# Two PSUM copies of q moved from VectorE to ScalarE, with another instruction order, in a fused attention and gated convolution kernel

## The chip, the cores and the metric

The kernel runs on one core of one Trainium2 chip. The metric is the device time of one execution in microseconds, as the median of several runs. All five engines of the core take part: TensorE (PE), VectorE (DVE), ScalarE (ACT), GpSimd (POOL), which only starts loads, and SyncE (SP), which only starts stores and the small copies through DRAM.

## The reference, cut to what matters

Eight batches, eight heads of 64 columns, 576 positions. First a linear attention without softmax, with an RMS norm per head; its result is the input of a feed-forward part with a convolution over positions and a gate:

```
kv  = einsum('bhsd,bhse->bhde', k, v)
o   = einsum('bhsd,bhde->bhse', q, kv)
o   = o / sqrt(mean(o*o, -1) + 1e-6) * g_norm          # per head
x   = o, heads side by side                            # (8, 576, 512)
h   = max(x @ w_in, 0)                                 # (8, 576, 1024)
c   = sum over k of conv_w[k] * h shifted by k-1       # 3 taps over positions
out = (h * sigmoid(c)) @ w_out                         # (8, 576, 512)
```

## The kernel before

The work is cut into some 660 small steps, each a function marked `@op` and named by two to four letters. A string `ORDER` lists all steps by name and numbers, such as `hm.3.2`; the kernel calls them in that order, and at the end ties every instruction to its predecessor on the same engine. So the string fixes the order on each engine and in each DMA queue, and semaphores do the rest: an engine that comes to a step whose input or buffer isn't ready waits, and everything behind it on that engine waits too. The strings are written out by a search outside of the kernel.

The steps, for batch b, pair of heads t (0 to 3), block f of 128 of the 1024 columns (0 to 7), with the engine of each:

- `Lq`, `Lk`, `Lv` (POOL) start the loads of a batch, two buffers each. Batch 0 is loaded in parts ahead of the order's steps.
- `qs` and `qt` (PE) transpose q into PSUM, `qs` one pair of batch 0, `qt.b.u` two pairs of a later batch; `qd` and `qc.b.u` copy the result to SBUF. These copies are of 128 x 576 and 128 x 1152 elements in bf16.
- `kv` (PE) multiplies k and v, and `kvc` copies the halves of the product into a block-diagonal matrix: on DVE for batch 0, on ACT for the others.
- `ot` (PE) makes o for a pair; `sq` (ACT) squares it and `oc` copies it to SBUF in the order of positions (ACT, for batch 0 mostly DVE).
- The norm. Batch 0: `on` (PE), `nl`, `nx` (ACT), `mu0` (DVE), pair by pair. Other batches, in the groups 1 (batch 1), 2 (batches 2 and 3), 3 (4 and 5), 4 (6 and 7): `ss` (PE) sums squares, `ln` and `ex` (ACT) give 1/rms. For groups 1 and 2, `sl` (DVE) splits it into bf16 parts, `sp` (PE) spreads it over partitions in PSUM and `mu` (DVE) multiplies. For groups 3 and 4 it goes through DRAM: `rw` (SP) writes it, `rr` (SP) reads it back spread over partitions, in two DMAs into one of four buffers rb, and `mr` (DVE) multiplies.
- `hm.b.f` (PE; `hs` its first three quarters) makes a block of h from all four pairs, `re` (ACT) applies the relu. `ws` (DVE) casts w_in, `cs` and `cm` (DVE) make constants for the norm.
- The convolution: `ta` and `ad` (DVE) make the taps and add them, `sg` (ACT) the sigmoid, `mg` (DVE) the gate. Two blocks of batch 0 have it on PE: `di`, `sv` (ACT), `cv` (PE), `mv` (DVE).
- `om.p.m` (PE) multiplies 128 rows of the pair p of batches with w_out, `ea` (ACT) copies the result to SBUF, `st` (SP) stores it.
- `wu.n` and `wa.n` (PE) are n matmuls of zeros which fill a wait.

PSUM has two pools. Pool a has three buffers of two banks and serves `ot`, `on`, `qt`, `hs`/`hm`, `sp`, `cv` and `wa`; pool b has two of one bank and serves `qs`, `kv`, `ss`, `om` and `wu`. A step on PE that takes a buffer waits for the last reader of what was in it.

Where a copy runs is decided by one function, from a default and from two tuples of exceptions, `ON_ACT` and `ON_DVE`:

```python
    def copy(token, on_dve, to, fr):
        if token in ON_DVE or on_dve and token not in ON_ACT:
            nc.vector.tensor_copy(to, fr)
        else:
            nc.scalar.activation(to, fr, AX.Copy)
```

Some lines of the profile are those of helpers: L237 and L239 are the DVE and the ACT copy above, L232 the load of an ACT table, L157 a load, L361 `qt`, L393 the larger matmul of `ot` and `on`, L435 `sq`, L510 `ln`, L526 `ex`, L554 `mu`, L571 `rr`, L580 `mr`, L595 `hm`, L608 `re`, L628 `ta`, L643 `sg`, L649 `mg`, L703 `om`, L710 `ea`, L721 `st`.

Of the kernel before, what the change touches and what calls it, by code (L numbers as in the profile page):

```python
# [65 lines left out]
ONES, KEEP, XB, RD, SQO, PW, ON_ACT, ON_DVE = ({0: (0, 1, 2, 3)}, ((0, 2), (0, 3)), (), (), (), (), ('oc.0.0',), ())  # L66

ORDER = """
cvq wu.11 qs.0.0 qd.0.0 cvk kv.0.0.1 kvc.0.0.1.0 kvc.0.0.1.1 cs wa.3 ot.0.0 oc.0.0 qs.0.1 kv.0.1.1 sq.0.0 wa.2
on.0.0 nl.0.0 kvc.0.1.1.1 kvc.0.1.1.0 qd.0.1 qs.0.2 wu.1 kv.0.2.1 qd.0.2 kvc.0.2.1.0 kvc.0.2.1.1 ot.0.1 wu.1  # L70
ot.0.2 sq.0.2 oc.0.1 nx.0.0 sd.0.1 wu.3 on.0.2 nl.0.2 Lq.1 nx.0.2 kv.0.3.1 mu0.0.0 kvc.0.3.1.0 kvc.0.3.1.1
qs.0.3 qd.0.3 on.0.1 nl.0.1 wa.4 ot.0.3 sq.0.3 mu0.0.2 cx cz ws.0 nx.0.1 mu0.0.1 wu.2 on.0.3 nl.0.3 nx.0.3
mu0.0.3 wu.5 hs.0.0 hs.0.1 hm.0.0 hm.0.1 re.0.1 re.0.0 Lk.1.0 Lv.1.0 Lk.1.1 ws.1 hm.0.2 hm.0.3 Lv.1.1 Lw Lq.2
Lk.2.2 re.0.2 ws.2 di.1 hm.0.7 qt.1.0 re.0.7 re.0.3 di.0 hm.0.6 re.0.6 hm.0.4 kv.1.0.2 qc.1.0 kvc.1.0.2.1
kvc.1.0.2.0 cm ta.0.2 re.0.4 hm.0.5 re.0.5 ot.1.1 sq.1.1 oc.1.1 ta.0.3 Lv.2.2 ad.0.1 qt.1.1 ot.1.0 oc.1.0
kv.1.2.2 kvc.1.2.2.1 cv.0.1 kvc.1.2.2.0 ta.0.6 qc.1.1 sq.1.0 ot.1.3 sq.1.3 ot.1.2 ta.0.7 ad.0.3 sq.1.2 wu.4
ss.1 oc.1.3 ln.1 ex.1 ta.0.4 sl.1 cv.0.0 ta.0.5 sv.0.0 sv.0.1 oc.1.2 wu.10 sp.1.0 mu.1.0 sp.1.1 sp.1.3 mu.1.1
mu.1.3 qt.2.1 sp.1.2 mu.1.2 qt.2.0 sg.0.1 sg.0.3 mg.0.3 qc.2.0 ad.0.2 hm.1.6 hm.1.7 re.1.6 qc.2.1 sg.0.2
mg.0.2 hm.1.4 hm.1.5 re.1.7 kv.2.0.4 re.1.5 kvc.2.0.4.0 kvc.2.0.4.1 re.1.4 hm.1.0 mg.0.1 ta.1.6 ta.1.7 mv.0.0
Lq.3 Lk.3.2 Lv.3.2 Lq.4 Lk.4.2 ot.2.3 oc.2.3 sq.2.3 hm.1.3 re.1.3 qt.3.1 re.1.0 ot.2.0 ot.2.1 oc.2.0 oc.2.1  # L80
ad.1.3 qc.3.1 sq.2.0 hm.1.2 ot.2.2 sq.2.1 qt.3.0 oc.2.2 sq.2.2 re.1.2 kv.3.0.4 hm.1.1 kvc.3.0.4.1 kvc.3.0.4.0
ot.3.2 re.1.1 ta.1.4 mv.0.1 ta.1.5 ad.1.2 qc.3.0 ot.3.1 sq.3.2 oc.3.2 sq.3.1 om.0.1 ta.1.2 ot.3.0 Lv.4.2
oc.3.1 ot.3.3 qt.4.1 sq.3.0 ss.2 ta.1.3 ad.1.1 sq.3.3 ss.3 qc.4.1 ea.0.1 ta.1.0 ta.1.1 ln.2 qt.4.0 qc.4.0
om.0.0 ex.2 om.0.3 sl.2 oc.3.3 oc.3.0 ea.0.0 ea.0.3 Lq.5 Lk.5.2 Lv.5.2 Lq.6 sp.2.0 sp.3.2 mu.2.0 sp.2.2 mu.3.2
mu.2.2 kv.4.0.4 sg.1.1 sg.1.3 sp.2.1 sp.2.3 om.0.2 sp.3.0 mu.2.3 mu.2.1 mg.1.1 kvc.4.0.4.1 mu.3.0 sp.3.3
hm.2.0 hm.2.3 sg.1.2 re.2.0 kvc.4.0.4.0 mu.3.3 Lk.6.2 mg.1.3 re.2.3 ea.0.2 sp.3.1 mu.3.1 hm.2.2 mg.1.2 re.2.2
ad.1.0 ot.4.0 sq.4.0 hm.3.2 oc.4.0 qt.5.1 kv.5.0.4 qc.5.1 re.3.2 sg.1.0 hm.3.3 kvc.5.0.4.0 ot.4.3 qt.5.0
re.3.3 ta.2.2 sq.4.3 hm.3.1 Lv.6.2 oc.4.3 kvc.5.0.4.1 mg.1.0 re.3.1 ot.4.1 qc.5.0 sq.4.1 oc.4.1 hm.3.0 hm.2.6
ta.2.3 ad.2.1 Lq.7 ot.5.2 re.3.0 re.2.6 hm.2.1 hm.2.7 oc.5.2 sq.5.2 re.2.1 ot.4.2 re.2.7 hm.3.6 st.0.2 oc.4.2
sq.4.2 hm.3.7 ta.2.0 ta.2.1 re.3.6 re.3.7 ot.5.3 hm.3.5 ot.5.0 sq.5.3 st.0.3 st.0.0 st.0.1 Lk.7.2 Lv.7.2  # L90
# [689 lines left out]
```

## Time and profile before

| | before |
|---|---|
| median of 3 runs (lowest to highest) | 189.31 us (189.17 to 190.07) |
| the profiled execution's own time | 190.19 us |
| its span in the profile | 187.9 us |
| PE busy | 178.5 us |
| DVE busy | 159.4 us |
| ACT busy | 150.2 us |
| moved by DMA | 32.35 MB |
| granted TensorE clock | 0.999 |

Busy time is the time in which an engine executes an instruction; matmuls overlap their successors in the record, so PE's figure is not a share of its peak. Rows of groups read: line, engine, operation, tiles, shapes, count, then total busy us and mean ns of one, then the idle time in front of them and what ended it. The chain that ended last is followed back from the last instruction, at each step to what released it; its rows are start, us, engine, tile and line. All times are from the start of the span.

### The profile page before, as it was taken

The page shows a single profiled execution, that of the slowest core. Times are in us where ns is not written, and L with a number is a line of the kernel's source. Part 1 is how long each engine was busy: PE and PEld are TensorE (multiplying, and loading weights), DVE is VectorE, ACT ScalarE, POOL GpSimd, SP SyncE. Part 2 cuts the span into 40 slices and gives each one's busy share as a digit, 9 for nine tenths or more (in the row PEclk, how much of TensorE's full clock was granted, in tenths as well). Part 3 has the DMA queues.
Part 4 walks back from the last instruction along what each step waited for, and adds up shares of the span by engine and source line. Part 5 has one row for each costly group of instructions (what it writes and reads, how often), then busy time and mean ns, then how long its engine had stood idle before and what let it go on. Part 6 is the DMA issues. An engine that isn't in the chain of part 4 may idle for free.

```text
span 187.9 us, 4432 instructions
## 1 busy us (share of the span) xinstructions
PE 178.5 (95%) x1787; PEld 108.0 (57%) x1787; DVE 159.4 (85%) x324; ACT 150.2 (80%) x233; POOL 29.3 (16%) x42
## 2 busy tenths in 40 slices
...
GB/s 147 183 265 332 203 205 204 206 202 203 204 204 203 207 200 238 265 205 128 118 178 196 198 131 61 0 89 262 161 232 178 98 81 3 108 128 129 166 195 167
DMA packets 30876, 32.35 MB, mean 172 GB/s; under 512 B 1776, under 2 KB 25864, under 8 KB 30856
## 3 DMA queue, kind: packets, MB, share of 16 engines
...
q14 instruction: 6, 0.05, 0.1%
...
## 4 chain that ended last, share of the span: by engine, by line
PE 47%; ACT 25%; DMA 9%; DVE 8%; SPq 4%; issue 2%; POOL 2%; ACTq 0%; POOLq 0%; DVEq 0%
PE om_ps L703 20%; PE h_ps L595 19%; ACT h L608 7%; DMA rb<-scr 6%; ACT sq L435 6%; ACT o L239 5%; SPq L571 3%; DMA v_sb<-in_v_dram 3%; PE kv_ps L319 2%; DVE h L649 2%; ACT L232 2%; ACT row L710 2%; DVE xT L580 2%; PE qt_ps L361 1%; DVE xT L554 1%
## 5 line engine op out<-in xcount | busy, mean ns | idle before, releaser
L595 PE MATMUL h_ps<-xT,w_in_sb 128*128 128x288 bf16 x512 | 68.4, 286 | 1.7 <-DVE xT L580 0.6
L703 PE MATMUL om_ps<-w_out_sb,h 128*128 128x512 bf16 (+1 forms) x296 | 64.4, 373 | 0.0
L595 PEld LDWEIGHTS <-w_in_sb 128*128 128x128 bf16 x512 | 49.3, 98 | 18.6 <-issue 4.1
L703 PEld LDWEIGHTS <-h 128*128 128x128 bf16 x296 | 28.5, 98 | 31.7 <-DVE h L649 0.3
L608 ACT ACTIVATE h<-h_ps 128x576 bf16<-128x576 f32 x64 | 40.1, 656 | 7.0 <-PE h_ps L595 6.6
L628 DVE TENSOR_SCALAR side<-h,cw 128x576 bf16<-128x576 bf16 (+1 forms) x92 | 38.2, 427 | 1.0
L643 ACT ACTIVATE tap<-tap 128x1152 bf16<-128x1152 bf16 (+1 forms) x23 | 34.1, 1496 | 2.3 <-DVE tap L637 2.3
L710 ACT ACTIVATE row<-om_ps 128x512 f32<-128x512 f32 (+1 forms) x37 | 21.5, 586 | 14.9 <-PE om_ps L703 13.6
L637 DVE TENSOR_TENSOR tap<-tap,side 128x1150 bf16<-128x1150 bf16 (+1 forms) x23 | 22.4, 973 | 0.8
L649 DVE TENSOR_TENSOR h<-h,tap 128x1152 bf16<-128x1152 bf16 (+1 forms) x23 | 21.6, 962 | 0.6 <-ACT tap L643 0.6
L636 DVE TENSOR_TENSOR tap<-tap,side 128x1150 bf16<-128x1150 bf16 (+1 forms) x23 | 22.1, 961 | 0.0
L435 ACT ACTIVATE sq<-o_ps 128x576 bf16<-128x576 f32 x31 | 19.7, 662 | 1.9 <-PE o_ps L393 1.9
L239 ACT ACTIVATE o<-o_ps 128x576 f32<-128x576 f32 x29 | 18.5, 657 | 1.8 <-PE o_ps L393 1.8
L628 DVE TENSOR_SCALAR tap<-h,cw 128x576 bf16<-128x576 bf16 (+1 forms) x46 | 19.3, 421 | 0.0
L580 DVE TENSOR_TENSOR xT<-o,rb 128x576 bf16<-128x576 f32 x16 | 12.0, 755 | 2.2 <-DMA rb<-scr 2.1
L237 DVE COPY qT<-qt_ps 128x1152 bf16<-128x1152 bf16 x14 | 10.5, 753 | 3.0 <-PE qt_ps L361 3.0
L728 PE MATMUL wu_ps<-zeros 128*128 128x512 bf16 x37 | 11.6, 454 | 1.2 <-DVE zeros L184 1.2
L157 POOL DMA_DIRECT2D q_sb<-in_q_dram x10 | 7.6, 756 | 33.1 <-PE qt_ps L361 32.2
L393 PE MATMUL o_ps<-qT,kvbd 128*128 128x512 bf16 x32 | 11.7, 379 | 0.0
L157 POOL DMA_DIRECT2D k_sb<-in_k_dram x11 | 9.1, 828 | 11.7 <-PE kv_ps L319 9.0
L361 PEld LDWEIGHTS <-q_sb 96*64 96x64 bf16 x336 | 8.3, 110 | 3.8 <-issue 3.4
L361 PE MATMUL qt_ps<-ident,q_sb 96*64 96x96 bf16 x336 | 9.6, 207 | 0.5 <-DVE xT L554 0.2
...
## 6 DMA issues: line engine op xcount, KB each, us to landing
...
```

Source lines behind the costliest of these rows:

```text
L239: nc.scalar.activation(to, fr, AX.Copy)
L361: nc.tensor.transpose(ps[i * D:(i + 1) * D, tt, r * PS:(r + 1) * PS], q_sb[:, 2 * (2 * u + tt) + i, r * D:(r + 1) * D], ident[:PS, :PS])
L435: nc.scalar.activation(to, fr, AX.Square)
L595: nc.tensor.matmul(ps[:, e, :HS], w_in_sb[:, t, f * P:(f + 1) * P], x[:, t, e * HS:(e + 1) * HS], start=(t == 0), stop=(t == NT - 1))
L608: nc.scalar.activation(h_tile(b // 2)[:, f, b % 2, :].rearrange("p (e n) -> p e n", e=2), T["hm", b, f][:, :, :HS], AX.Relu)
L628: nc.vector.tensor_scalar_mul(tap[m][:, f % 2, :, :].rearrange("p b s -> p (b s)"), h_tile(p)[:, f, bs, :].rearrange("p b s -> p (b s)"), ...
L636: nc.vector.tensor_add(tap[:, :, 1:], tap[:, :, 1:], side[:, 0, :, :S - 1])
L637: nc.vector.tensor_add(tap[:, :, :S - 1], tap[:, :, :S - 1], side[:, 1, :, 1:])
L643: nc.scalar.activation(tap, tap, AX.Sigmoid)
L649: nc.vector.tensor_mul(h, h, T["tap", c, j])
L703: nc.tensor.matmul(to, h[:, f, m * P:(m + 1) * P], w_out_sb[:, f, cols], start=(f == 0), stop=(f == NF - 1))
L710: nc.scalar.activation(T["os", p, m][:, cols], fr, AX.Copy)
```

## The change

Two tokens are added to `ON_ACT`, so that the copies `qc.1.0` and `qc.1.1` (128 x 1152 bf16, PSUM to SBUF) are ACT instructions and no longer DVE instructions. The whole `ORDER` is another one: nearly the same steps (only the fillers `wu` and `wa` are cut up differently: 37 matmuls in `wu` and 9 in `wa` before, 42 and 4 after), in other places. Two new tuples, `F32` and `OM_A`, are empty. The parts of the order that the text below speaks of:

```diff
-ONES, KEEP, XB, RD, SQO, PW, ON_ACT, ON_DVE = ({0: (0, 1, 2, 3)}, ((0, 2), (0, 3)), (), (), (), (), ('oc.0.0',), ())
+ONES, KEEP, XB, RD, SQO, PW, ON_ACT, ON_DVE, F32, OM_A = ({0: (0, 1, 2, 3)}, ((0, 2), (0, 3)), (), (), (), (), ('oc.0.0', 'qc.1.0', 'qc.1.1'), (), (), ())
 
 ORDER = """
-cvq wu.11 qs.0.0 qd.0.0 cvk kv.0.0.1 kvc.0.0.1.0 kvc.0.0.1.1 cs wa.3 ot.0.0 oc.0.0 qs.0.1 kv.0.1.1 sq.0.0 wa.2
-on.0.0 nl.0.0 kvc.0.1.1.1 kvc.0.1.1.0 qd.0.1 qs.0.2 wu.1 kv.0.2.1 qd.0.2 kvc.0.2.1.0 kvc.0.2.1.1 ot.0.1 wu.1
-ot.0.2 sq.0.2 oc.0.1 nx.0.0 sd.0.1 wu.3 on.0.2 nl.0.2 Lq.1 nx.0.2 kv.0.3.1 mu0.0.0 kvc.0.3.1.0 kvc.0.3.1.1
-qs.0.3 qd.0.3 on.0.1 nl.0.1 wa.4 ot.0.3 sq.0.3 mu0.0.2 cx cz ws.0 nx.0.1 mu0.0.1 wu.2 on.0.3 nl.0.3 nx.0.3
-mu0.0.3 wu.5 hs.0.0 hs.0.1 hm.0.0 hm.0.1 re.0.1 re.0.0 Lk.1.0 Lv.1.0 Lk.1.1 ws.1 hm.0.2 hm.0.3 Lv.1.1 Lw Lq.2
-Lk.2.2 re.0.2 ws.2 di.1 hm.0.7 qt.1.0 re.0.7 re.0.3 di.0 hm.0.6 re.0.6 hm.0.4 kv.1.0.2 qc.1.0 kvc.1.0.2.1
-kvc.1.0.2.0 cm ta.0.2 re.0.4 hm.0.5 re.0.5 ot.1.1 sq.1.1 oc.1.1 ta.0.3 Lv.2.2 ad.0.1 qt.1.1 ot.1.0 oc.1.0
-kv.1.2.2 kvc.1.2.2.1 cv.0.1 kvc.1.2.2.0 ta.0.6 qc.1.1 sq.1.0 ot.1.3 sq.1.3 ot.1.2 ta.0.7 ad.0.3 sq.1.2 wu.4
-ss.1 oc.1.3 ln.1 ex.1 ta.0.4 sl.1 cv.0.0 ta.0.5 sv.0.0 sv.0.1 oc.1.2 wu.10 sp.1.0 mu.1.0 sp.1.1 sp.1.3 mu.1.1
-mu.1.3 qt.2.1 sp.1.2 mu.1.2 qt.2.0 sg.0.1 sg.0.3 mg.0.3 qc.2.0 ad.0.2 hm.1.6 hm.1.7 re.1.6 qc.2.1 sg.0.2
...
-Lq.3 Lk.3.2 Lv.3.2 Lq.4 Lk.4.2 ot.2.3 oc.2.3 sq.2.3 hm.1.3 re.1.3 qt.3.1 re.1.0 ot.2.0 ot.2.1 oc.2.0 oc.2.1
-ad.1.3 qc.3.1 sq.2.0 hm.1.2 ot.2.2 sq.2.1 qt.3.0 oc.2.2 sq.2.2 re.1.2 kv.3.0.4 hm.1.1 kvc.3.0.4.1 kvc.3.0.4.0
-ot.3.2 re.1.1 ta.1.4 mv.0.1 ta.1.5 ad.1.2 qc.3.0 ot.3.1 sq.3.2 oc.3.2 sq.3.1 om.0.1 ta.1.2 ot.3.0 Lv.4.2
-oc.3.1 ot.3.3 qt.4.1 sq.3.0 ss.2 ta.1.3 ad.1.1 sq.3.3 ss.3 qc.4.1 ea.0.1 ta.1.0 ta.1.1 ln.2 qt.4.0 qc.4.0
-om.0.0 ex.2 om.0.3 sl.2 oc.3.3 oc.3.0 ea.0.0 ea.0.3 Lq.5 Lk.5.2 Lv.5.2 Lq.6 sp.2.0 sp.3.2 mu.2.0 sp.2.2 mu.3.2
-mu.2.2 kv.4.0.4 sg.1.1 sg.1.3 sp.2.1 sp.2.3 om.0.2 sp.3.0 mu.2.3 mu.2.1 mg.1.1 kvc.4.0.4.1 mu.3.0 sp.3.3
...
-oc.5.3 re.3.5 sq.5.0 ss.4 ot.5.1 hm.2.4 sq.5.1 ss.5 oc.5.0 om.0.7 ad.2.0 re.2.4 ta.2.6 ta.2.7 ad.2.3 hm.3.4
-ln.3 ex.3 oc.5.1 hm.2.5 re.3.4 rw.3 ea.0.7 re.2.5 st.0.7 qt.6.0 qt.6.1 sg.2.3 rr.4.0 om.0.4 ea.0.4 om.0.8
-ea.0.8 ta.2.4 ta.2.5 ad.2.2 qc.6.1 qt.7.1 sg.2.1 kv.6.0.4 om.0.6 mr.4.0 qt.7.0 rr.4.2 qc.6.0 kvc.6.0.4.1
-mr.4.2 kvc.6.0.4.0 kv.7.0.4 ea.0.6 rr.4.1 sg.2.2 mr.4.1 qc.7.0 rr.4.3 mr.4.3 qc.7.1 ot.6.2 mg.2.3 rr.5.0
...
-sq.6.1 re.5.7 ot.7.2 oc.6.1 ad.3.0 ea.1.5 sq.7.2 ss.6 st.1.0 re.5.4 hm.4.4 re.4.4 ss.7 ln.4 ex.4 hm.5.5 hm.5.2
-om.1.7 re.5.5 hm.5.3 ta.3.6 ta.3.7 oc.7.2 ad.3.3 ta.3.4 hm.4.3 re.5.2 hm.4.2 om.1.2 sg.3.3 ta.3.5 ad.3.2
-ea.1.7 mg.3.3 rw.4 rr.6.0 rr.6.2 st.1.5 st.1.7 rr.6.3 re.4.2 ta.3.2 re.5.3 om.1.4 ea.1.2 re.4.3 om.1.3 ea.1.4
-mr.6.0 ta.3.3 sg.3.0 st.1.4 ea.1.3 mr.6.2 rr.6.1 st.1.3 om.1.8 ea.1.8 sg.3.2 ad.3.1 om.1.1 om.1.6 rr.7.3
-rr.7.1 mr.6.3 mr.6.1 mg.3.0 sg.3.1 hm.6.0 hm.6.5 mg.3.2 hm.6.1 re.6.0 ta.4.0 ea.1.1 re.6.1 mr.7.1 rr.7.0
...
+cvq wu.11 qs.0.0 qd.0.0 cvk kv.0.0.1 kvc.0.0.1.0 kvc.0.0.1.1 wa.3 ot.0.0 sq.0.0 qs.0.1 oc.0.0 cm qd.0.1
+kv.0.1.1 Lq.1 kvc.0.1.1.1 kvc.0.1.1.0 wa.1 qs.0.2 qd.0.2 ot.0.1 on.0.0 oc.0.1 kv.0.2.1 kvc.0.2.1.1 kvc.0.2.1.0
+nl.0.0 sd.0.1 nx.0.0 qs.0.3 ot.0.2 on.0.1 Lk.1.0 Lv.1.0 Lk.1.1 Lv.1.1 Lw kv.0.3.1 qd.0.3 sq.0.2 nl.0.1
+kvc.0.3.1.1 on.0.2 nl.0.2 kvc.0.3.1.0 cx cz mu0.0.0 ot.0.3 sq.0.3 wu.4 on.0.3 nx.0.2 nx.0.1 ws.0 mu0.0.2
+mu0.0.1 ws.1 nl.0.3 nx.0.3 mu0.0.3 di.1 ws.2 Lq.2 wu.8 hs.0.0 Lk.2.2 hs.0.1 hm.0.0 hm.0.1 hm.0.2 re.0.0 hm.0.3
+re.0.2 re.0.1 di.0 hm.0.7 re.0.3 hm.0.6 re.0.6 ta.0.2 qt.1.0 qc.1.0 re.0.7 hm.0.4 re.0.4 hm.0.5 re.0.5
+kv.1.0.2 kvc.1.0.2.0 kvc.1.0.2.1 qt.1.1 qc.1.1 wu.1 ot.1.1 sq.1.1 ot.1.0 oc.1.1 oc.1.0 ta.0.3 ad.0.1 ta.0.6
+wu.4 kv.1.2.2 ta.0.7 ad.0.3 kvc.1.2.2.0 kvc.1.2.2.1 cv.0.0 sq.1.0 cs ot.1.3 sq.1.3 ta.0.4 ta.0.5 ad.0.2 ot.1.2
+sq.1.2 oc.1.3 wu.4 ss.1 ln.1 ex.1 cv.0.1 sv.0.1 sv.0.0 oc.1.2 sl.1 wu.10 sp.1.1 mu.1.1 sg.0.1 sp.1.0 mu.1.0
+sp.1.3 qt.2.0 mu.1.3 sg.0.2 sp.1.2 mu.1.2 qt.2.1 qc.2.1 hm.1.4 re.1.4 hm.1.0 re.1.0 Lv.2.2 qc.2.0 mg.0.1
+mv.0.1 mv.0.0 hm.1.1 hm.1.2 sg.0.3 re.1.1 re.1.2 kv.2.0.4 hm.1.5 kvc.2.0.4.1 kvc.2.0.4.0 re.1.5 ot.2.1 ot.2.0
+mg.0.2 ta.1.0 ta.1.1 mg.0.3 ad.1.0 om.0.3 sq.2.0 ta.1.4 ta.1.5 oc.2.0 sq.2.1 ot.2.2 Lq.3 Lk.3.2 Lv.3.2 Lq.4
+ot.2.3 oc.2.1 oc.2.3 sq.2.3 oc.2.2 sq.2.2 hm.1.7 hm.1.3 re.1.3 Lk.4.2 qt.3.1 ad.1.2 qc.3.1 qt.3.0 kv.3.0.4
+Lv.4.2 qc.3.0 hm.1.6 re.1.7 ea.0.3 kvc.3.0.4.1 kvc.3.0.4.0 ot.3.3 re.1.6 Lq.5 ot.3.0 sq.3.3 Lk.5.2 om.0.1
+ot.3.1 ta.1.2 ta.1.3 ad.1.1 oc.3.0 oc.3.3 sq.3.0 ot.3.2 sq.3.1 sq.3.2 ta.1.6 ea.0.1 qt.4.1 ss.2 st.0.3 ss.3
+ln.2 ex.2 qc.4.1 ta.1.7 ad.1.3 qt.4.0 om.0.2 ea.0.2 oc.3.1 oc.3.2 sl.2 om.0.0 sp.2.0 sp.2.3 qc.4.0 sp.2.1
+sg.1.3 sg.1.2 Lv.5.2 kv.4.0.4 mu.2.0 mu.2.1 mu.2.3 kvc.4.0.4.0 sp.2.2 mu.2.2 sp.3.1 sp.3.2 kvc.4.0.4.1 sg.1.0
...
+sq.4.1 re.3.1 oc.4.1 om.0.6 ss.4 st.0.0 oc.5.1 ss.5 ln.3 hm.3.4 ta.2.0 re.3.4 ex.3 hm.2.4 re.2.4 ea.0.6 ta.2.1
+ad.2.0 hm.3.5 re.3.5 ta.2.4 hm.2.5 re.2.5 qt.7.1 ta.2.5 st.0.7 st.0.1 qt.6.0 qt.7.0 qc.6.0 sg.2.3 om.0.8 rw.3
+rr.4.0 qc.7.0 ad.2.2 ea.0.8 qt.6.1 om.0.4 rr.4.2 kv.6.0.4 sg.2.0 ea.0.4 Lv.7.2 kvc.6.0.4.0 kv.7.0.4 mr.4.0
+kvc.6.0.4.1 qc.6.1 sg.2.1 sg.2.2 mr.4.2 rr.4.1 mr.4.1 ot.6.2 rr.4.3 mr.4.3 om.0.5 rr.5.0 hm.4.0 re.4.0 st.0.4
+kvc.7.0.4.1 qc.7.1 hm.4.5 re.4.5 hm.4.4 oc.6.2 re.4.4 kvc.7.0.4.0 mg.2.3 rr.5.1 sq.6.2 hm.4.6 re.4.6 mr.5.0
...
+sq.7.2 oc.7.0 oc.6.0 ss.6 ss.7 st.1.1 ta.3.6 ta.3.7 ln.4 hm.5.4 re.5.4 ex.4 oc.7.2 st.0.5 hm.5.5 re.5.5 om.1.2
+ad.3.3 hm.4.2 ea.1.2 hm.5.2 rw.4 st.0.8 ta.3.4 ta.3.5 ad.3.2 hm.5.3 sg.3.0 re.4.2 ea.1.3 om.1.6 re.5.2 rr.6.0
+rr.6.3 hm.4.3 mg.3.0 ta.3.2 re.5.3 re.4.3 ea.1.6 mr.6.0 st.1.2 om.1.4 rr.6.2 om.1.8 ea.1.4 ta.3.3 rr.6.1
+st.1.6 om.1.5 mr.6.3 sg.3.2 ad.3.1 mr.6.2 ea.1.8 st.1.4 mr.6.1 rr.7.3 mg.3.2 ea.1.5 sg.3.3 om.1.0 st.1.8
+mg.3.3 om.1.7 hm.6.0 hm.6.1 sg.3.1 re.6.0 ta.4.0 re.6.1 mg.3.1 hm.6.4 hm.6.6 ea.1.0 hm.6.3 re.6.6 re.6.4
...
 """
...
+    spread32 = consts.tile([P, NT * 2, 2, D], FP32, name="spread32") if F32 else None
...
     @op
     def Lw():
+        if F32:
...
         ps = ps_a.tile([P, 2, 512], FP32, name="sp_ps", tag="a")
         T["sp", b, t] = ps
+        if g in F32:
...
+            return
...
+        elif (p, m) in OM_A:
+            ps = ps_a.tile([P, 2, 512], FP32, name="om2_ps", tag="a")
+            parts = [(ps[:, 0], slice(0, D_model))]
```

## The prediction

> **What bounds the kernel now.** I read the page's busy shares first, then the busy time by 10 us stretches, the chain that ended last, and the waits. Columns of the stretches: from:to, length, then PE, PEld, DVE, ACT, POOL busy (instructions), PE clock, DMA share, GB/s.
>
> ```profile
> PE 178.5 (95%) x1787; PEld 108.0 (57%) x1787; DVE 159.4 (85%) x324; ACT 150.2 (80%) x233; POOL 29.3 (16%) x42
> ...
> 20.00:30.00 10.00, 9.80 (x155) 7.37 (x154) 7.21 (x20) 8.59 (x19) 3.14 (x4) 1.00 1.29 204
> 30.00:40.00 10.00, 9.10 (x99) 4.98 (x97) 9.36 (x21) 8.85 (x14) 1.84 (x3) 1.00 1.30 204
> 40.00:50.00 10.00, 9.15 (x128) 6.29 (x127) 9.37 (x20) 8.10 (x14) 1.83 (x3) 1.00 1.32 204
> ...
> 80.00:90.00 10.00, 9.89 (x85) 6.06 (x85) 9.82 (x16) 9.90 (x18) 0.00 (x0) 1.00 0.99 154
> ```
>
> From about 45 us to the end three engines are full together. PE's share overstates it, so I price PE from dense runs in the chain:
>
> ```profile
> 30.56 1.70 ACT sq L435 x3
> 32.26 0.54 ACT o L239
> 32.82 0.51 ACT rs L510
> ...
> 131.36 4.92 DMA rb<-scr
> 136.33 0.04 issue
> 136.38 0.77 DVE xT L580
> 137.19 7.76 PE h_ps L595 x62
> 144.94 3.45 PE om_ps L703 x16
> 148.40 7.95 PE h_ps L595 x64
> 156.35 27.66 PE om_ps L703 x136
> ```
>
> 64 hm matmuls in 7.95 us are 0.124 each, so one hm (8 matmuls) costs PE 1.0 us; one om (8 x 512 columns) 1.72 us. From 137.19 to the end nothing on PE waits. Its losses lie before: some 1.6 us in all at 40 to 51 us, and about 1.6 us where the rows of rs come back through DRAM, 101 to 107 us (0.8) and at 136.4 to 137.2 (0.8). At 27 to 33 us the chain runs over ACT. The waits that matter:
>
> ```profile
> ACT h L608 <- PE h_ps L595: 6.6, 10, 1.6
> ...
> DVE xT L580 <- DMA rb<-scr: 2.1, 5, 0.6
> ```
>
> ACT has idle time only early: the timeline shows 1.58 us before 20.19, 0.44, 0.76, then 1.43 and 0.95 at 39 to 42, and next to none from 44 to 137.
>
> **What the Trainium skill says.** "Perfetto Trace Analysis", section "Identifying the Most-Contended Engine", warns that matmul busy time doesn't measure headroom, as matmuls are pipelined; here a 288-column matmul is recorded as 286 ns but issues every 124, so I agree. "TensorE: Matmul & The Clock Gate", section "Wait — 56ns, not 53.3ns?", gives columns / 2.4 GHz + 2.5 ns: 122.5 ns for 288, against the 124 measured. "ScalarE: Activation LUTs", section "What ACT_TABLE_LOAD costs", prices an ACTIVATE with immediate scale and bias at 186 + 0.833 N ns, overlapping its neighbour by 93. For 576 that is 666; the trace has 656. For the new copy of 1152 elements it gives 1146 alone, 1053 in a row (an estimate; no row of the trace has this copy).
>
> **The change part by part.** I walk the new order by hand with durations and start-to-start distances of the trace (relu, sq or oc 0.54, sigmoid of 1152 1.10, kvc of two pairs 0.27, ta 0.84, ad 1.57, mu 0.70, qc on DVE 0.75), adding 0.1 to 0.15 us from a producer's end to its consumer, and give PE's lag against before at equal work done.
>
> *Copies.* Removed: qc.1.0 and qc.1.1 on DVE, row "L237 DVE COPY qT<-qt_ps 128x1152", 753 ns, 2 x 0.75 = 1.5 us. Added on ACT: 2 x 1.06 = 2.1 us. Bounds: 2 x 0.95 (all overlap) to 2 x 1.3. Behind qc.1.0 on ACT wait re.0.7, re.0.4 and re.0.5, behind qc.1.1 sq.1.1, oc.1.1, oc.1.0 and kvc.1.2; PE waits for those to get its PSUM buffers back, and for kvc.1.2 before ot.1.3.
>
> *Start, to hs.0.0.* Fewer fillers (wu and wa 27 against 32), qs.0.3 and qd.0.3 moved before kv.0.3, cs (1.65 us of DVE) moved out and cm (0.45) in. The landing of the last v part at 13.45 is unmoved, POOL's 24 loads keep their order. From it: kv.0.3 13.6, kvc to 14.45, ot.0.3 14.5 (before 15.56), sq.0.3 15.0, nx.0.1 to 16.85, mu0.0.1 to 17.7, hs.0.0 at 17.75 against 18.03. Lag -0.3. Fillers hide in these waits.
>
> *Batch 1, to the first hm.1.* di.1 now precedes re.0.0 on ACT and re.0.2 precedes re.0.1, so ACT still waits 0.55 and 0.75 us; then it is full: re.0.3 23.0, qc.1.0 24.5, re.0.5 26.85, qc.1.1 27.95, oc.1.0 to 30.65, kvc.1.2 to 31.2, sq.1.2 to 32.85. ss.1 follows, ln.1 at 33.5 where before has 32.82. So of the 2.1 us, ACT's old idle time takes 1.1 and the earlier start 0.3; +0.7 remains. The four fillers (19 matmuls of 0.215 = 4.1 us, 3.0 before) stand in PE's waits for ACT and cost nothing; if that cover were gone, the extra 1.1 would be paid. From there each step keeps its distance: first hm.1 at 39.9 against 39.20. Lag +0.7.
>
> *40 to 57 us.* Before, PE loses 0.35 us apiece in front of hm.1.3, ot.2.1, hm.1.2, qt.3.0 because ACT and DVE return buffers late. Now ad.0.2 was done before sl.1, so mg.0.3 comes sooner and om.0.3 (1.72 us of PE) stands among batch 2's ot. It finishes at 47.95; at 54.65 the same hm, kv, ot and qt are done as before at 53.85, plus om.0.3: +0.8 - 1.7. Lag -0.9.
>
> *Norm of batches 2 and 3, 60 to 70 us.* qt.3.1 comes late for DVE (1 us idle at 51), and ta.1.6, ta.1.7, ad.1.3 and qc.4.0 (4.0 us) now stand round sl.2: sl.2 at 61.05 (60.17), the first mu at 63.6 (62.44). All four om of pair 0 were spent earlier, so PE waits on mu after mu for buffers: 0.5 + 0.45 + 0.45 + 0.1 = 1.5 us. hm.2.6 ends at 68.9 where before has two hm.2 done at 68.4. Lag +0.5; DVE about +0.2, since ad.1.0 is behind it.
>
> *Rows through DRAM, batches 4 and 5.* Between ss.5 and hm.4.0 PE has 4 hm + 4 qt + 3 om + 2 kv + 1 ot = 13.5 us of cover, before 15.0. ss.5 is 1.7 later, its table load already over; rw.3 at 90.5 (89.13). On SP st.0.7 left the place between rw.3 and rr.4.0 (0.2 us). Before, rw.3 to the last mr.4 takes 12.05, so now 11.85: 102.35; hm.4.0's last quarter is reached at 102.6. No stall. DVE waits 1.3 us among mr.4, but the fillers moved apart (mg.2.1 between mr.5.0 and mr.5.1) spare the 0.8 us among mr.5, and st.0.4 between rr.5.0 and rr.5.1 falls in a wait for an rb buffer. PE's 0.8 us falls to 0.2. Lag -0.1.
>
> *Batches 6 and 7.* rr.6.1 was behind st.1.5, st.1.7 and st.1.4; ea.1.4 held it to 130.73 and it landed 4.9 us on. Now only st.1.2 is before it: it can be issued by 129, landed by 133. DVE is then the limit: 0.6 us of waiting goes, mr.6.1 ends at 136.6; stall 0.2 to 0.4 for 0.8. Lag -0.5. After it the work is the same list reordered (16 hm, 17 om, the halved last om), 47 us; DVE's last mg ends 0.25 us before PE reaches its first om of batch 7, as before. Cost 0, from -0.2 to +0.8.
>
> *Nothing:* F32 and OM_A are empty, so the code behind them emits nothing.
>
> Sum: -0.3 + 1.0 - 1.6 + 1.4 - 0.6 - 0.4 = **-0.5 us**. The profiled execution took 190.19 (span 187.9 + 2.29), giving 189.7; it lies 0.88 above the median of the runs, so on the median 189.31 - 0.5 = 188.8. A difference of 0.5%, 0.95 us, is about what a measurement of this kernel can tell from none.
>
> **Rivals.** *R1, the norm of 2 and 3 isn't DVE's.* If mu starts 1 us sooner than I walked (ad.1.3 fitting in DVE's idle us at 51), the +1.4 goes: -1.9, 187.4. For it: ACT's and DVE's early idle time, 4 us, is what a reorder can fill; against: DVE 9.06 of 10 busy at 60 to 70. *R2, slower: hm.4.0 waits for rb.* The cover there is 1.5 us shorter and my slack is 0.25. It decides at rw.3 later than 90.75: each further us is paid whole by PE. ACT is full there (9.90 of 10), so the 2.1 us put on ACT may still be owed, with sq.4.1 now the last square and oc.4.1, oc.5.1 in front of ln.3: two of these and the table load (2 x 0.54 + 1.28 = 2.4) no longer hidden puts rw.3 at 92.3, less what mr.5 gives back (0.7): +1.3, 190.6. For it: rb landed just in time in before; against: ss.5 comes later on PE than ACT needs. *R3, nothing:* PE is full either way, all shifts fall into waits: 189.3; it lies inside the first case.
>
> **How the numbers follow.** First case 0.45, its own range 188.0 to 189.6 (copies at either bound, hand errors); R1 0.30; R2 0.25. Faster by over 0.5% (below 188.36): 0.12 of the first and 0.28 of R1, 0.40. Within: 0.33 + 0.02 + 0.05 = 0.40. Slower: 0.20 of R2. Range 186.8 to 190.8, R1 and R2 with 0.2 to 0.6 us more at the ends.
>
> **What would show it.** Right: two ACT copies of 1.1 to 1.2 us about 24.5 and 28; ln.1 near 33.5; PE denser at 40 to 57; PE waiting on mu at 63 to 67; no wait of DVE for rb near 136. Wrong: hm.4.0 starting behind rb (R2), sp.2 dense (R1), or ln.1 past 34.5, which would mean that the copies are not absorbed at all.

## The result and the profile after

The changed kernel is slower: 191.88 us (190.93 to 193.29, six runs) against 189.69 (188.82 to 190.48) for the kernel before beside it, a ratio of 1.0128 with a 95% interval of 1.0084 to 1.0173. The forecast was 188.8, at most 190.8.

The profiled execution of after took 190.93 us (span 189.1, so 1.83 outside it; before 187.9 and 2.29). That is 0.74 over before's profiled one, while the medians differ by 2.19: before's profiled execution was 0.50 above its median, after's 0.95 below. So there are two questions: where 0.74 us went in the profile where -0.5 was forecast, and why the median lies higher still.

The changed file is longer, so its line numbers differ from those named above: L239 is now the DVE copy and L241 the ACT copy, L317 `ws`, L328 `kv`, L370 `qt`, L401 and L402 `ot`, L444 `sq`, L519 `ln`, L547 `sl`, L563 `sp`, L569 `mu`, L595 `mr`, L610 `hm`, L623 `re`, L658 `sg`, L721 `om`, L728 `ea`. All the kernels below but e1 have these numbers.

The page's busy line, and four stretches of 10 us (columns as in those of before):

```profile
PE 176.7 (93%) x1787; PEld 107.9 (57%) x1787; DVE 158.2 (84%) x322; ACT 152.7 (81%) x235; POOL 28.4 (15%) x42
```

```profile
20.00:30.00 10.00, 8.92 (x143) 6.05 (x142) 9.21 (x20) 8.33 (x16) 2.77 (x3) 1.00 1.29 204
...
40.00:50.00 10.00, 9.69 (x113) 6.69 (x113) 9.76 (x23) 7.99 (x15) 2.30 (x3) 1.00 1.32 204
...
60.00:70.00 10.00, 9.20 (x110) 5.34 (x109) 9.17 (x16) 9.57 (x15) 2.30 (x3) 1.00 1.30 215
...
100.00:110.00 10.00, 9.37 (x66) 6.22 (x67) 8.00 (x11) 9.93 (x14) 0.00 (x0) 1.00 0.55 172
```

ACT is 2.5 us busier over the span (152.7 for 150.2), 2.26 of it the two copies; PE is denser at 40 to 50 (9.69 for 9.15) and thinner at 20 to 30 (8.92 for 9.80), at 60 to 70 (9.20 for 10.00) and at 100 to 110 (9.37 for 9.67). The chain that ended last (start, us, what) shows the new start and the unchanged end:

```profile
9.67 10.85 DMA w_stage<-in_moe_w_in_dram
20.54 1.30 DVE w_in_sb L317
21.88 2.15 PE h_ps L610 x16
...
28.16 1.13 ACT qT L241
...
121.14 0.51 ACT rs L519
121.69 1.89 PE om_ps L721 x8
...
138.01 7.84 PE h_ps L610 x64
...
157.15 27.66 PE om_ps L721 x136
```

From 138.01 on PE waits for nothing, as before from 137.19. Early on the chain now runs over the load of w_in, and PE waits 0.97 us there for `ws`; in before that load was not in the chain. The waits (engine and line, what for, us, times, longest):

```profile
ACT h L623 <- PE h_ps L610: 10.5, 15, 1.7
...
DVE w_in_sb L317 <- DMA w_stage<-in_moe_w_in_dram: 2.4, 1, 2.4
DVE xT L595 <- DMA rb<-scr: 2.0, 3, 0.8
```

ACT waits longer for PE (6.6 before), DVE has a new wait for w_in, and the wait for rb is as large as ever (2.1 before). PE's own waits late in the kernel, from its timeline (start, us, operation, then the wait in front and what ended it):

```profile
99.04 0.95 PE L328 MATMUL kv_ps<-v_sb,k_sb 96*64 96x64 bf16 x48 [0.47 <-ACT row L728]
...
104.52 3.30 PE L610 MATMUL h_ps<-xT,w_in_sb 128*128 128x288 bf16 x24 [0.50 <-ACT h L623]
...
121.69 1.89 PE L721 MATMUL om_ps<-w_out_sb,h 128*128 128x512 bf16 x8 [0.24 <-ACT rs L519]
```

All three end on ACT. What ACT does there, from its timeline:

```profile
96.39 2.11 ACT L658 ACTIVATE tap<-tap 128x2304 bf16<-128x2304 bf16 x1
98.40 0.59 ACT L728 ACTIVATE row<-om_ps 128x512 f32<-128x512 f32 x1
98.88 0.75 ACT L241 ACTIVATE kvbd<-kv_ps 64x256 bf16<-64x256 f32 x2
99.66 4.14 ACT L658 ACTIVATE tap<-tap 128x2304 bf16<-128x2304 bf16 x2
103.82 0.65 ACT L623 ACTIVATE h<-h_ps 128x576 bf16<-128x576 f32 x1
```

Sigmoids of 2.1 us stand in front of the short ACT steps that return PSUM buffers: kv.7 waits for ea.0.4 behind sg.2.0, hm.4.4 for re.4.0 behind sg.2.1 and sg.2.2 (ot.6.2 still holds the third buffer of pool a).

**PE's lag by stage.** To place gains and losses I add up PE's work along each kernel's own list (hm 0.98 us, om 1.725, ot 0.245, qt 0.59, kv 0.76, and so on, from dense runs), read from the timelines when each group starts, and take the difference to before at equal work; a positive lag means that the kernel is behind before. The numbers are good to about 0.2 us, and each comes from one profiled execution. The columns are kernels explained below; rows are before's time.

| before's time | after | e7 | e6 | e13 | e12 |
|---|---|---|---|---|---|
| 25 us | -0.2 | -0.5 | +0.2 | -0.2 | -0.9 |
| 40 us | +0.9 | +0.7 | +0.2 | +0.9 | +0.2 |
| 58 us | -1.1 | +0.1 | -0.2 | +0.4 | -1.8 |
| 70 us | +1.0 | +0.1 | +1.9 | +0.4 | +0.6 |
| 99 us | -0.1 | +0.1 | +0.8 | +0.3 | -0.7 |
| 112 us | +0.9 | -0.4 | +1.5 | +1.0 | +0.6 |
| 127 us | +1.5 | -0.1 | +2.1 | +1.6 | +0.7 |
| 158 us | +0.8 | -0.6 | +1.6 | +1.0 | +0.1 |

Of the fall from 127 to 158 us, 0.56 us is before's: in its profiled execution hm.6.0 takes 1.54 us (136.38 to 137.92) for the 0.98 of a dense run, because mr.6.1 waits 0.61 us for rb. e7 has before's list there and no such wait; its eight hm.6 run in one piece:

```profile
136.06 8.11 PE L610 MATMUL h_ps<-xT,w_in_sb 128*128 128x288 bf16 x64
```

### The profile page after: what moved, and what is told of

Same layout as the page of the kernel before. It is cut to its first block, busy times and chain, and to the rows that moved or that the text cites. A ratio compares the mean times of both kernels' runs of the same rounds, so it can differ in the third digit from the quotient of the medians.

```text
span 189.1 us, 4433 instructions
## 1 busy us (share of the span) xinstructions
PE 176.7 (93%) x1787; PEld 107.9 (57%) x1787; DVE 158.2 (84%) x322; ACT 152.7 (81%) x235; POOL 28.4 (15%) x42
## 4 chain that ended last, share of the span: by engine, by line
PE 52%; ACT 21%; DMA 10%; DVE 5%; POOL 4%; issue 2%; SPq 2%; ACTq 0%; POOLq 0%; DVEq 0%
PE om_ps L721 25%; PE h_ps L610 20%; DMA w_stage<-in_moe_w_in_dram 6%; ACT o L241 5%; ACT sq L444 5%; ACT h L623 4%; DMA rb<-scr 4%; ACT L234 2%; SPq L586 2%; DVE xT L595 2%; PE qt_ps L370 2%; PE wu_ps L746 2%; ACT tap L658 2%; DVE xT L569 2%; POOL v_sb L159 1%
## 5 line engine op out<-in xcount | busy, mean ns | idle before, releaser
L610 PE MATMUL h_ps<-xT,w_in_sb 128*128 128x288 bf16 x512 | 67.4, 286 | 2.5 <-DVE w_in_sb L317 1.0
L721 PE MATMUL om_ps<-w_out_sb,h 128*128 128x512 bf16 (+1 forms) x296 | 64.7, 373 | 0.2 <-ACT rs L519 0.2
L610 PEld LDWEIGHTS <-w_in_sb 128*128 128x128 bf16 x512 | 49.6, 98 | 19.2 <-issue 3.8
L623 ACT ACTIVATE h<-h_ps 128x576 bf16<-128x576 f32 x64 | 40.3, 655 | 11.0 <-PE h_ps L610 10.5
L721 PEld LDWEIGHTS <-h 128*128 128x128 bf16 x296 | 28.7, 98 | 31.7 <-issue 0.6
L658 ACT ACTIVATE tap<-tap 128x1152 bf16<-128x1152 bf16 (+1 forms) x23 | 33.9, 1495 | 0.1
L728 ACT ACTIVATE row<-om_ps 128x512 f32<-128x512 f32 (+1 forms) x37 | 21.6, 592 | 12.6 <-PE om_ps L721 10.3
L444 ACT ACTIVATE sq<-o_ps 128x576 bf16<-128x576 f32 x31 | 19.7, 674 | 2.8 <-PE o_ps L402 2.8
L241 ACT ACTIVATE o<-o_ps 128x576 f32<-128x576 f32 x29 | 18.5, 674 | 0.0
L595 DVE TENSOR_TENSOR xT<-o,rb 128x576 bf16<-128x576 f32 x16 | 11.8, 751 | 2.0 <-DMA rb<-scr 2.0
L402 PE MATMUL o_ps<-qT,kvbd 128*128 128x512 bf16 x32 | 11.1, 380 | 0.0
L159 POOL DMA_DIRECT2D k_sb<-in_k_dram x11 | 8.4, 767 | 13.4 <-PE kv_ps L328 10.3
L239 DVE COPY qT<-qt_ps 128x1152 bf16<-128x1152 bf16 x12 | 8.8, 753 | 1.5 <-PE qt_ps L370 1.5
L328 PE MATMUL kv_ps<-v_sb,k_sb 96*64 96x64 bf16 x384 | 8.3, 197 | 1.7 <-DMA v_sb<-in_v_dram 1.0
L370 PEld LDWEIGHTS <-q_sb 96*64 96x64 bf16 x336 | 8.1, 110 | 2.7 <-issue 2.5
```

Of the source, the lines that this page charges most:

```text
L159: nc.gpsimd.dma_start(out=qkv[name, b][:, h0:h0 + n, :], in_=src[b, h0:h0 + n].rearrange("h (p r) d -> p h (r d)", r=R))
L444: nc.scalar.activation(to, fr, AX.Square)
L610: nc.tensor.matmul(ps[:, e, :HS], w_in_sb[:, t, f * P:(f + 1) * P], x[:, t, e * HS:(e + 1) * HS], start=(t == 0), stop=(t == NT - 1))
L623: nc.scalar.activation(h_tile(b // 2)[:, f, b % 2, :].rearrange("p (e n) -> p e n", e=2), T["hm", b, f][:, :, :HS], AX.Relu)
L658: nc.scalar.activation(tap, tap, AX.Sigmoid)
L721: nc.tensor.matmul(to, h[:, f, m * P:(m + 1) * P], w_out_sb[:, f, cols], start=(f == 0), stop=(f == NF - 1))
```

## The experiments

Ratios are to the kernel before on the same chip, with 95% intervals; e0 to e3 ran together, and so did each later set of four, and the last two. Before's median moved between 189.47 and 190.11 us from set to set, so ratios are compared and not times.

### The copies, the order, the fillers

**e0_after** is the changed kernel again.

> The changed kernel again, on the chip and beside the runs of the three others. Clock theory (TensorE idles more during batch 0, so in part of the executions its granted clock falls, and 1.4 us of the 2.2 us between the medians is that): the executions differ in granted clock, those under 0.99 are slowest, ratio 1.008 to 1.016. Order theory (all of the loss is waits on the way from hm.4.0 to hm.6.0 and in batch 1, the same in every execution): executions within 0.3% of each other, ratio near 1.005, as between the two profiled executions.

Measured: 191.42 us, 1.0093 (1.0057 to 1.0128). Of the twelve executions of after in both sets, five had a granted TensorE clock of 0.994 or more and took 190.74 to 191.14; seven had 0.977 to 0.991 and took 191.62 to 193.29, their median 192.34. The medians of the two groups are 1.46 us apart. All sixteen of before beside them had 0.995 or more.

**e3_fill** adds six filler matmuls to after's start:

```diff
- ... oc.0.1 kv.0.2.1 ... nx.0.0 qs.0.3 ... Lw kv.0.3.1
+ ... oc.0.1 wu.2 kv.0.2.1 ... nx.0.0 wu.2 qs.0.3 ... Lw wu.2 kv.0.3.1
```

> The changed kernel with six more matmuls of zeros in TensorE's three waits during batch 0 (two each before kv.0.2, qs.0.3 and kv.0.3), 52 in all against 46. Clock theory: the granted clock is 0.995 or more in every execution, and the ratio falls to 1.002 to 1.006. Order theory: no change, the ratio stays at that of the changed kernel in the same job, or 0.1% above it.

Measured: 190.93 us (190.63 to 192.54), 1.0060 (1.0034 to 1.0087); the interval overlaps e0's, so the gain isn't proved by the time, though the median is where after's executions at full clock are (190.74 to 191.14). The clock is plainer: 0.995 or more in all seven executions, and 0.990 or more in every later kernel that has these fillers. Its slowest execution, 192.54 us at a clock of 0.995, was the one profiled. On DVE the third scaling of w_in stands in it like this:

```profile
21.55 1.29 DVE L317 TENSOR_SCALAR w_in_sb<-w_stage,cw 128x2048 bf16<-128x2048 f32 x1 [2.46 <-DMA w_stage<-in_moe_w_in_dram]
```

That is 1.0 us later than in the profile of after, and hm.0.7 with it (22.89 for 21.88).

**e1_copies** is before with the two copies on ACT and nothing else:

```diff
-... (), ('oc.0.0',), ())
+... (), ('oc.0.0', 'qc.1.0', 'qc.1.1'), ())
```

> The kernel before with its own order, and only the two copies qc.1.0 and qc.1.1 moved to ScalarE. Copies theory (2.1 us of ScalarE work in the stretch where ScalarE sets the pace are not absorbed): ratio 1.006 to 1.012, ln.1 about 1.5 us later than 32.8. Order theory (the copies are taken up by ScalarE's idle time, the new order is what costs): ratio 0.997 to 1.005, ln.1 no more than 0.9 us later.

Measured: 191.06 us, 1.0055 (1.0033 to 1.0077), about 1.05 us. The two copies took 1.13 and 1.11 us on ACT. On PE's timeline:

```profile
32.02 0.19 PE L392 MATMUL o_ps<-qT,kvbd 128*128 128x64 bf16 x1 [1.22 <-ACT qT L239]
```

ot.1.3 waits for the second copy, ln.1 comes at 34.23 (32.82 before) and the 1.4 us stay to the end of the span. In before's order 1.4 of the 2.24 us are thus not absorbed; the ratio lies between the two expectations.

**e2_order** is after with the copies back on DVE.

> The new order, with the two copies left on VectorE. Order theory: still slower than before, ratio 1.006 to 1.014, since the stalls at hm.4, hm.5 and the low clock stay. Copies theory: ratio 0.995 to 1.003, ln.1 at about 32.5 in place of 33.7.

Measured: 197.59 us, 1.0409 (1.0374 to 1.0444), far from both expectations. DVE's timeline, then PE's, then the stretch at 40 us:

```profile
25.73 0.76 DVE L239 COPY qT<-qt_ps 128x1152 bf16<-128x1152 bf16 x1 [1.97 <-PE qt_ps L370]
28.96 0.76 DVE L239 COPY qT<-qt_ps 128x1152 bf16<-128x1152 bf16 x1 [2.48 <-PE qt_ps L370]
```

```profile
42.08 1.62 PE L563 MATMUL sp_ps<-wparts,spread 128*128 128x288 bf16 x6 [4.89 <-DVE wparts L547]
```

```profile
40.00:50.00 10.00, 7.92 (x78) 5.38 (x79) 8.21 (x15) 2.26 (x3) 0.77 (x1) 0.66 1.29 194
```

In their place in the new order the copies make DVE wait 4.5 us for PE, everything up to sl.1 comes late, PE stands for 4.89 us, and the mean clock from 40 to 50 us is 0.66. The Trainium skill ("TensorE: Matmul & The Clock Gate", section "What's actually happening") says that the clock halves after about 3.4 us without work; this trace agrees: the clock is 0.80 from 41 to 42 us, still inside the wait, and 0.50 from 42 to 48. So copies and order can't be told apart by swapping them whole: the new order was made for copies on ACT.

This profile shows something else too. Up to the first of the two copies, at 25 us, e2's list and engines are after's, and in this start it caught a fall of the clock:

```profile
10.00:14.00 4.00, 2.61 (x46) 1.45 (x44) 2.78 (x8) 2.70 (x4) 3.81 (x6) 1.00 1.19 291
...
16.00:17.00 1.00, 1.00 (x5) 0.45 (x4) 0.82 (x2) 0.72 (x2) 0.53 (x2) 0.50 0.98 373
```

From 14 to 15 us the mean clock is 0.64 and from 17 to 18 us 0.65, so it was 0.50 from about 14.3 to 17.7 us. Over 10 to 14 us, just ahead of it, PE was busy for 2.61 of 4 us. In the profiles of after and e0 it was 2.74 and 2.61, in those of before and e3 3.54 and 3.59; in none of these four did the clock fall there.

### Which part of the order loses

**e7_early** has after's list (with e3's fillers, copies on ACT) up to qc.2.1, then before's from hm.1.6. **e6_late** is the mirror: before's list with its copies on DVE up to ad.0.2, then after's from hm.1.4.

> The mirror of it: the kernel after up to qc.2.1 (its start with the six extra fillers, both copies on ScalarE), and from hm.1.6 on the order of the kernel before. Theory S: about as slow as after with its fillers, 190.8 (190.5 to 191.1). Theory R: 189.8 to 190.1. If both halves are slow, order after 40 us matters only together with what was done before it.

> The kernel before up to its ad.0.2 (so its start, its batch 1 and the copies on DVE), and from hm.1.4 on the order of the kernel after. Theory S (the loss lies in the start and batch 1, and the later order neither gains nor loses): 189.7 (189.4 to 190.0), level with before. The forecast's own walk of the stages after 40 us (-1.5 us) says 188.3. Theory R (the later order loses at 100 to 112 us): 190.3 to 190.8.

Measured: e7 189.83 us, 1.0014 (0.9994 to 1.0035), level with before; e6 191.71 us, 1.0124 (1.0086 to 1.0161), as slow as after. The theory that the loss lies in the start falls: the start with both copies costs nothing that can be measured once before's rest follows. The table shows it: e7's lag of 0.7 at 40 us is 0.1 by 58. The order after 40 us is what loses, and it loses with and without the copies.

**e4_wsplit** takes e3_fill and splits the last load of w_in, so that hm.0.7 needs half of it only:

```diff
-    W_COLS = ((0, 256), (256, 512), (512, 1024))
+    W_COLS = ((0, 256), (256, 512), (768, 1024), (512, 768))
...
-    for i in range(3):
+    for i in range(4):
...
-... ws.2 ...
+... ws.2 ws.3 ...
```

> The kernel with the six extra fillers, and in it the last 1 MB part of w_in split into two loads of 512 KB, columns 768 to 1023 first, each with its own scaling on DVE. Theory L (landing): in the new order PE reaches hm.0.7 at 21.7 us, and the landing of the last part (20.4 to 21.5 us, plus 1.3 us of scaling) sets its start from there on; executions in which it lands late are the slow ones at full clock. Expected: no wait of DVE for w_stage in front of the third scaling over 0.3 us, hm.0.7 right behind hm.0.3, median 190.5 (190.2 to 190.8) where the fillers alone gave 190.93, and no run over 191.2. Rival A: ScalarE, with the two copies, sets the pace of this stage; then an earlier hm.0.7 only lengthens ScalarE's queue and the median stays at 190.8 to 191.0.

Measured: 190.71 us (190.21 to 191.24), 1.0062 (1.0040 to 1.0085). hm.0.7 now stands right behind hm.0.3, as theory L has it, and the slowest execution took 191.24 where it allowed 191.2; the median moved too little to tell, and the ratio, 1.0060 in e3, not at all.

**e5_rb** is e3_fill with three edits in the stage of batches 4 and 5:

```diff
-... qc.6.1 sg.2.1 sg.2.2 mr.4.2 ... rr.5.0 hm.4.0 re.4.0 st.0.4 ... re.4.5 hm.4.4 oc.6.2 ... sq.6.2 ... rr.5.2 ...
+... qc.6.1 sg.2.1 mr.4.2 ... rr.5.0 oc.6.2 hm.4.0 re.4.0 sq.6.2 ... re.4.5 sg.2.2 hm.4.4 ... rr.5.2 st.0.4 ...
```

> The kernel with the six extra fillers, with the stage of batches 4 and 5 mended: on SP st.0.4 behind rr.5.2 (in front of it rr.5.1, rr.5.3 and rr.5.2 waited 1.8 us), on ACT the second of the two sigmoids of batch 2/3 behind re.4.5, oc.6.2 and sq.6.2 in front. Theory R (the stage between rows and hm.4 is where the expected gain went): DVE's waits for rb among mr.5 fall from 2.0 us to under 0.4, PE's waits between 101 and 112 us from about 0.9 to under 0.3, median 190.3 (190.1 to 190.6) against 190.93. Rival A (ScalarE is full and merely pays later): the same waits go, and PE loses as much between 112 and 137 us; median 190.8 to 191.0.

Measured: 191.58 us, 1.0108 (1.0074 to 1.0143): worse. On PE's timeline:

```profile
102.17 5.06 PE L610 MATMUL h_ps<-xT,w_in_sb 128*128 128x288 bf16 x40
108.49 0.20 PE L401 MATMUL o_ps<-qT,kvbd 128*128 128x64 bf16 x1 [1.25 <-ACT kvbd L241]
```

With ot.6.2's buffer emptied early, five hm run without the 0.50 us wait. But the sigmoid now stands in front of kvc.7, and ot.7.3 waits 1.25 us. DVE's waits for rb were still 1.4 us (2.0 in after, 2.3 in e3).

### ScalarE's share

ACT is never idle for more than some hundredths of a us in 5 from 75 to 105 us, in before and in after alike. e8 to e11 ask whether PE's place there is simply ACT's work done.

**e9_actplus** is e7 with two idle ACT copies (`nz`, behind re.3.6 and behind sg.2.2).

> The kernel with the start of after and the rest of before (189.83), and in it two idle ScalarE copies of 128 x 512 (estimated 0.6 us each, zeros into a scratch tile that nobody reads), one behind re.3.6 near 80 us and one behind sg.2.2 near 104 us. Theory A: ScalarE is full there, so the time rises by what they take, 1.0 to 1.2 us, to 190.9 (190.7 to 191.2). If TensorE is the bound there and ScalarE has slack, as the forecast's sum had it: no change, 189.7 to 190.0.

Measured: 190.96 us, 1.0046 (1.0020 to 1.0071), that is 0.0032 or 0.6 us over e7, with intervals that just overlap. The two took 635 ns each, 1.27 us: about half of it reached the end. By ratio that is between the two expectations.

**e8_ocdve** is e4 with oc.6.2 and oc.7.3 on DVE, oc.6.2 moved behind mg.2.1.

> The kernel with the split load of w_in, and in it two ScalarE copies of o (oc.6.2, oc.7.3, 0.54 us each) given to VectorE, into its waits for rb at 105 to 109 us. Theory A (from 75 to 130 us ScalarE never idles, so that PE's place at 130 us is ScalarE's ledger and nothing else): ScalarE is 1.1 us of work further at 110 us, PE's waits for it go, and the time falls by about 0.9, from 190.71 to 189.8 (189.5 to 190.1). Rival R (the rows through DRAM, SP's issue times and VectorE's waits for rb bind there): the two copies delay mr.5 by up to 0.3 us, 190.6 to 191.0.

Measured: 191.65 us, 1.0079 (1.0053 to 1.0104), slower than either theory had it in time; the interval overlaps e4's. DVE's line, then PE's:

```profile
107.72 0.76 DVE L239 COPY o<-o_ps 128x576 f32<-128x576 f32 x1 [1.40 <-ACT sq L444]
```

```profile
111.20 0.65 PE L610 MATMUL h_ps<-xT,w_in_sb 128*128 128x288 bf16 x4 [1.04 <-DVE xT L595]
```

The copy on DVE waited for the square on ACT, which reads the same PSUM buffer and stands ahead of it in the list; mr.5.1 behind it came that much later. So this run is no test of ACT; it shows that mr.5 has no slack of 1.4 us, since PE paid 1.04.

**e10_om03** is e4 with om.0.3 behind ot.3.3 (as in before, after batch 2's ot) and ea.0.3 behind re.1.6.

> The kernel with the split load of w_in, and in it om.0.3 moved from among the ot of batch 2 (46.5 us) to behind ot.3.3 (about 54 us), as before has it, its copy ea.0.3 behind re.1.6. Theory A: om.0.3 at 46.5 us gives ScalarE nothing to do for 1.7 us, and ScalarE then idles 0.99 us at 50 to 55 us (0.19 in before); moved, that idle time falls to under 0.3 us and the time falls with it, to 190.0 (189.8 to 190.3) from 190.71. Theory of the forecast (TensorE's lead counts): the 0.9 us that om.0.3 won at 40 to 55 us is lost again, 190.7 to 191.5.

Measured: 192.34 us, 1.0116 (1.0091 to 1.0141), so 0.0054, about 1.0 us, worse than e4. PE's timeline:

```profile
46.89 0.19 PE L401 MATMUL o_ps<-qT,kvbd 128*128 128x64 bf16 x1 [0.25 <-ACT h L623]
...
47.98 0.19 PE L401 MATMUL o_ps<-qT,kvbd 128*128 128x64 bf16 x1 [0.68 <-ACT o L241]
...
49.06 2.23 PE L610 MATMUL h_ps<-xT,w_in_sb 128*128 128x288 bf16 x16 [0.68 <-ACT o L241]
```

Without om.0.3 PE waits 1.6 us for ACT in the same place. The forecast's step at 40 to 57 us holds, with a loss a little larger than it had allowed, and theory A is wrong here.

**e11_both** joins e8 and e10.

> Both edits together: om.0.3 behind ot.3.3, and oc.6.2 and oc.7.3 on VectorE in its waits for rb. Theory A: the two gains add, 189.1 (188.8 to 189.5), below before (189.6). If only one of the two engines' shares counts: 189.8 to 190.2. Neither: 190.7.

Measured: 193.26 us, 1.0164 (1.0139 to 1.0189), which no theory had: 0.0102 over e4, where the two edits alone show 0.0017 and 0.0054. No gain of ACT's comes out of joining them.

### The stage from the rows on

**e13_cut** is e7 up to ex.3 and has the steps that are left in after's order from there; **e12_cut** is e4 up to ex.3 and has the rest in before's order (ea.0.6 early).

> The mirror of it: the kernel with the start of after and before's order (ratio 1.0014) up to its ex.3, and from there on the order of after. Theory O: it loses at 100 to 127 us what after loses, about 1.2 us, ratio 1.007 to 1.009. Theory F: the cover is there, ratio 1.000 to 1.003.

> The kernel with the split load of w_in up to its ex.3 (about 91 us), and from there on the order of the kernel before (ea.0.6 kept early). Theory O (the new order of the stage from the rows of batches 4/5 on is itself worse: sigmoids in front of the ScalarE copies that give TensorE its buffers back, st.0.4 in front of rr.5.1, norm of 6/7): TensorE's lag of 0.4 us at 99 us is all that is left, ratio to before 1.000 to 1.003 against 1.0062. Theory F (the om that were spent early are missing as cover, and ss.5 comes later, so the rows land too late whatever follows): TensorE waits as long there, ratio 1.005 to 1.010.

Measured: e13 191.08 us, 1.0084 (1.0053 to 1.0115); e12 190.27 us, 1.0044 (1.0028 to 1.0061). e13 is where theory O puts it. Its PE timeline has after's three waits again:

```profile
99.28 0.95 PE L328 MATMUL kv_ps<-v_sb,k_sb 96*64 96x64 bf16 x48 [0.33 <-ACT row L728]
...
104.76 3.30 PE L610 MATMUL h_ps<-xT,w_in_sb 128*128 128x288 bf16 x24 [0.50 <-ACT h L623]
...
121.82 1.89 PE L721 MATMUL om_ps<-w_out_sb,h 128*128 128x512 bf16 x8 [0.24 <-ACT rs L519]
```

e12 falls just between the two theories. Its PE timeline shows why:

```profile
99.57 0.20 PE L401 MATMUL o_ps<-qT,kvbd 128*128 128x64 bf16 x1 [0.83 <-ACT kvbd L241]
...
103.17 0.41 PE L610 MATMUL h_ps<-xT,w_in_sb 128*128 128x288 bf16 x2 [0.73 <-DVE xT L595]
103.84 5.12 PE L610 MATMUL h_ps<-xT,w_in_sb 128*128 128x288 bf16 x40 [0.26 <-DVE qT L239]
```

Here hm.4.0 does stall behind mr.4 (0.73 us): with three om left as cover in place of five, PE arrives before the rows. Ahead of it ot.6.2 waits 0.83 us for kvc.6, which stands behind sg.2.1 on ACT. From 104 us on e12 loses little. In the table, from 99 to 127 us:

| list up to ex.3 | list from ex.3 | kernel | lag gained, 99 to 127 us |
|---|---|---|---|
| before's | before's | e7 | -0.2 |
| before's | after's | e13 | +1.3 |
| after's | before's | e12 | +1.4 |
| after's | after's | after | +1.6 |

So both theories hold in part, and the losses don't add: whichever half is after's, the stage costs 1.3 to 1.6 us, and only before's two halves fit each other. For e13 the times say so too (its interval is clear of e7's); e12's interval overlaps e4's. Where before's list stands, in e7, ACT empties ot.6.2's buffer between two sigmoids, and PE runs six hm in one piece. Its ACT timeline, then its PE timeline:

```profile
98.93 2.11 ACT L658 ACTIVATE tap<-tap 128x2304 bf16<-128x2304 bf16 x1
100.95 0.63 ACT L241 ACTIVATE o<-o_ps 128x576 f32<-128x576 f32 x1
101.48 0.64 ACT L444 ACTIVATE sq<-o_ps 128x576 bf16<-128x576 f32 x1
102.01 2.12 ACT L658 ACTIVATE tap<-tap 128x2304 bf16<-128x2304 bf16 x1
```

```profile
101.47 6.48 PE L610 MATMUL h_ps<-xT,w_in_sb 128*128 128x288 bf16 x48
```

**e14_st** is e4 with st.0.4 behind rr.5.2 on SP.

> The kernel with the split load of w_in, and st.0.4 behind rr.5.2 on SP, nothing else. Theory R (SP's 1.8 us for st.0.4 and its wait make rb late for mr.5): VectorE's waits for rb among mr.5 fall from 1.3 to 2.0 us to under 0.7, TensorE gains 0.2 to 0.4 us, ratio 1.004 to 1.005 against 1.0062. Otherwise (ScalarE holds TensorE there) no change, 1.006.

Measured: 190.53 us, 1.0050 (1.0033 to 1.0067), inside theory R's range but not to be told from e4. DVE's waits for rb were 0.84 and 0.68 us, no less than in e4 (1.2 in all), and PE kept the waits for ACT. The queue step alone isn't the cause.

**e15_cand** is e7 with e4's split load.

> The kernel with the start of after (both copies on ScalarE, six extra fillers) and the order of before from hm.1.6 on (ratio 1.0014), and in it the split load of w_in, so that no late landing holds hm.0.7. Expected: the slow runs of that start (190.4 to 191.6) go, ratio 0.998 to 1.001. If the landing doesn't matter there: 1.001 to 1.002.

Measured: 189.60 us (189.14 to 190.23), 1.0011 (0.9991 to 1.0031): level with before, as e7. Its slow executions are gone (e7's highest was 191.60), as expected if they were late landings of w_in. No version here beats before.

**e16_kv** is e14 with kv.6 and kv.7 in front of om.0.4 and their four copies in front of sg.2.0; **e17_kvoc** is the same with oc.6.2 and oc.7.3 on DVE, ahead of their squares.

```diff
-om.0.4 rr.4.2 kv.6.0.4 sg.2.0 ea.0.4 Lv.7.2 kvc.6.0.4.0 kv.7.0.4 mr.4.0 kvc.6.0.4.1 qc.6.1 ...
+Lv.7.2 kv.6.0.4 rr.4.2 kvc.6.0.4.0 kvc.6.0.4.1 kv.7.0.4 om.0.4 kvc.7.0.4.1 kvc.7.0.4.0 sg.2.0 ea.0.4 mr.4.0 qc.6.1 ...
```

> The kernel with the split load of w_in and st.0.4 behind rr.5.2 (ratio 1.005), and in it TensorE's wait at kv.7 (0.47 us, for ea.0.4 behind a 2.1 us sigmoid) taken away: kv.6 and kv.7 in front of om.0.4 on TensorE, the four copies of kv.6 and kv.7 in front of sg.2.0 on ScalarE. Theory O (single waits from an unlucky order): the 0.47 us is won and stays won, ratio 1.002 to 1.003. Theory A (ScalarE has no idle time from 75 to 130 us, so each wait taken away comes back at the next buffer): hm.4.4's wait grows from 0.50 to 0.8 to 1.0 us, ratio 1.004 to 1.006.

> The same, and oc.6.2 and oc.7.3 (1.08 us of ScalarE) on VectorE in front of their squares, in VectorE's waits for rb (0.84 and 0.68 us), so that nothing of mr.5 comes later than now. Theory A: ScalarE's work falls by 1.1 us in its full stretch and TensorE's waits at 104 to 127 us with it, ratio 0.999 to 1.002. Theory O: as e16_kv, no further gain.

Measured: e16 191.39 us, 1.0074 (1.0045 to 1.0103); e17 191.83 us, 1.0104 (1.0059 to 1.0149). PE's timeline in e16, then in e17:

```profile
105.57 3.10 PE L610 MATMUL h_ps<-xT,w_in_sb 128*128 128x288 bf16 x24 [0.91 <-ACT h L623]
```

```profile
105.56 3.10 PE L610 MATMUL h_ps<-xT,w_in_sb 128*128 128x288 bf16 x24 [1.52 <-ACT h L623]
109.39 2.12 PE L610 MATMUL h_ps<-xT,w_in_sb 128*128 128x288 bf16 x16 [0.71 <-ACT h L623]
```

kv.7's wait is gone in both and hm.4.4's is 0.91 and 1.52 us for 0.50. In e16 it came back as theory A said, and the time is even higher. But e17 has 1.1 us less on ACT and is no faster: ACT then idles 1.35 us between 105 and 110 (0.69, 0.33 and 0.33, each until PE has finished an hm). As I read the list, ot.6.2 holds one of the three buffers of pool a until its copy on DVE (106.63) and its square (109.24) are done, so that hm and re take turns on the other two. So neither single waits nor ACT's sum of work alone holds PE here; the order in which the buffers come back seems to count too.

## Why the prediction was wrong

**The sum.** On the profiled executions the forecast said -0.5 and they show +0.74. By its own steps, with PE's lag after each:

| step | forecast | measured |
|---|---|---|
| start and batch 1, to 40 us | +0.7 | +0.9 |
| 40 to 57 us | -1.6 | -2.0 |
| norm of groups 2 and 3 | +1.4 | +2.1 |
| 70 to 99 us | no step | -1.1 |
| rows of batches 4 and 5, 99 to 112 us | -0.6 | +1.0 |
| 112 to 127 us | no step | +0.6 |
| rows of batches 6 and 7, 127 to 158 us | -0.4 | -0.7 |
| the end, and outside the span | 0 | -0.1 |

The last row holds the 0.46 us less outside the span and about 0.4 us more between 158 us and the span's end; the rows add up to the measured +0.74 within the accuracy of the lags.

**What held.** Two ACT copies of 1.13 us, ln.1 at 33.74 (forecast 33.5), first hm.1 at 40.12 (39.9), rw.3 at 90.49 (90.5), the last mr.4 done at 101.57 (102.35), hm.4.0 at 101.90 with no stall (101.8). The value of om.0.3 as a filler was confirmed by e10. The copies were absorbed where after's start is used (e7); e1, where 1.4 of the 2.24 us are not, shows that this is for the larger part the new order's doing and not idle time that was there anyway. At 63 to 67 us R1 didn't come: the norm stage was dearer than walked, not free.

**What failed: "PE's 0.8 us falls to 0.2".** This step, the rows of batches 4 and 5, stands in the sum with -0.6 us; PE lost 1.0 us by 112 us and 0.6 more by 127. It was worked out from one question, when the rows land, and on that it was right: hm.4.0 didn't wait for them. What it left out is that PE there takes PSUM buffers that ACT returns, and that ACT has 2.1 us sigmoids in its list. The new list puts sg.2.0 in front of ea.0.4, and sg.2.1 and sg.2.2 together in front of re.4.0: waits of 0.47 and 0.50 us, and 0.24 for ln.4, 1.2 of the 1.6 us. I had the tokens in the diff and priced none of the three. The swap in e13 shows that this list brings the loss by itself. That the loss is these waits is read from the traces: where e5 and e16 took one of them away, another grew, and the time didn't fall.

**Right in number, not shown to be the list's doing: "stall 0.2 to 0.4 for 0.8".** In after rr.6.1's rows are there in time and the stall in front of hm.6.0 is gone. But e7 doesn't have it either, with before's list, so it may belong to before's one profiled execution. The 0.8 was also read too large: PE's start at 136.38 and its next at 137.19 are 0.81 apart, with two matmuls between them, so the stall was 0.56.

**R2** had its place right. Its mechanism, cover that is missing so that hm.4.0 waits for mr.4, is at work in e12 (0.73 us), where before's list follows, and not in after. Its number doesn't follow from its own terms: rw.3 at 92.3 is 1.55 us past the 90.75 that it names, and with the rest of the sum that makes about +1.0 and not +1.3. After's loss at the same place came in another way. Both belong to the question that R2 asked, what the early om cost later, and I gave it 0.25.

**From profile to median.** "It lies 0.88 above the median of the runs, so on the median 189.31 - 0.5" took the shift to be the same for both kernels. After's executions spread more than before's, and the larger share of the spread goes with the granted clock: 1.46 us between the two groups. "Fillers hide in these waits" was thus wrong in a way the sum didn't have: PE's clock depends on the fillers ahead of hs.0.0 (27 matmuls for 32), and six more bring it back. No profile of after caught a fall, but e2's did, in the same start: half speed from 14.3 to 17.7 us. By estimate such a fall lowers the mean clock over 190 us by 0.009, to 0.991 as in the mildest of the seven, and costs PE 1.7 us if it has work throughout, near the 1.46 us. The second cause, the landing of the last part of w_in, is seen: at 20.5 us it already takes away most of the earlier start (-1.2 us at hs.0.0, -0.2 at 25 us), and at 21.5 in e3's profile it costs 1.0 more. The forecast had walked the start to hs.0.0 only, one load short.

**What stays open.** Whether the seven slower executions of after fell where e2 fell. Whether any list can keep after's lead at 58 us and not pay it back at 100 to 127 us. e5, e16 and e17 took single waits away, and each came back elsewhere. Also open is why PE wins 1.1 us between 70 and 99 us, where no single wait of before's is longer than 0.2 us, and what the 0.4 us at 112 to 127 us are that ln.4 doesn't explain. Without that unforeseen gain of 1.1 us the forecast would have missed by more.
